# Attention and channel mix on one core: the second chunk in whole float32, and new due dates for the first four chunks

## The chip, the core and the metric

The kernel runs on one core of a Trainium2 chip. The core has a matrix engine (TensorE, "PE" in the profile, with its weight loads "PEld" shown apart), VectorE (DVE), ScalarE (ACT), GpSimd (POOL), and SyncE (SP), which here issues all loads and stores. The engines run side by side, each through its own queue in order, and wait for one another by semaphores. The metric is the device time of one execution in microseconds, lower is better. A difference of about 0.5% is what a measurement of this kernel can tell.

## The reference

Inputs q, k, v are 8 batches by 8 heads by 576 tokens by 64, in float32. Keys and values are averaged over groups of 8 tokens, so each head has 72 keys. Then comes a channel mix with weights w_k (512 x 1024), w_v (1024 x 512) and w_r (512 x 512):

```python
k_p = k.reshape(B, H, Sp, pool, D).mean(axis=3)
v_p = v.reshape(B, H, Sp, pool, D).mean(axis=3)
scores = scale * np.matmul(q, k_p.transpose(0, 1, 3, 2))
attn = softmax(scores)                     # written out in the reference
x = np.matmul(attn, v_p)                   # to [B, S, 512]
x_prev = np.concatenate([np.zeros((B, 1, D)), x[:, :-1, :]], axis=1)
xk = mu_k * x + (1.0 - mu_k) * x_prev
xr = mu_r * x + (1.0 - mu_r) * x_prev
k = np.maximum(xk @ w_k, 0.0)
v = k * k @ w_v
r = 1.0 / (1.0 + np.exp(-(xr @ w_r)))
out = (r * v).astype(np.float32)
```

## The kernel before

**Tiles and chunks.** The 4608 tokens are 36 tiles of 128 for attention and 13 chunks for the channel mix: chunk 0 has 128 tokens (tile 0), chunk 1 has 256 (tiles 1 and 2), the other eleven 384 (three tiles each).

**Stages of one chunk.** Scores and softmax per tile (`softmax`, `part`; `BY_HEAD` names the parts whose exponentials are taken head by head on ACT with the row sum beside it, in place of a subtraction and a row sum on DVE); `transposed` and `transposed_rest` turn the weights of a tile over; `attended` (L937) multiplies by the values for each of 4 groups of 128 channels; `shifted` (L950) and `joined` (L990) blend each token with the one before; `x_parts` (L1006, L1008) splits the result; `hidden` (L1034) multiplies by w_k in 8 blocks and squares the ReLU (L1043, L1050, then split at L1056 and L1058); `gate` (L1082) multiplies by w_r; `mixed` (L1115) multiplies by w_v; L1125 multiplies the two and L1129 stores.

**Two kinds of product.** A split product writes each operand as a high and a low part in float32r and runs three matmuls (high x high, low x high, high x low). A whole product is one matmul on plain float32, shown as two records. Chunk 0 is whole throughout (`WHOLE`), chunk 1 in the attention alone (`WHOLE_ATT`), everything else is split. In chunk 0, `joined` and `hidden` write their results straight into the operand, so there is nothing to split.

**Weights.** The 20 blocks of w_k, w_r and w_v arrive as pairs of words. `convert` rebuilds the float32 block in place (one ACT instruction, L528, two DVE instructions, L530 and L533). `split` then makes the high part on ACT (L555) and the low part on DVE or POOL (L558, by `LOW_BY`). There are 21 buffers for blocks; each split takes a new one and leaves the rebuilt block's to the next, so the splits run one after another in the order of the loads. A split waits for chunk 0's last use of the rebuilt block.

**Loads.** SP issues in the order of `LOADS`: k and v halves of a batch (two each), r (the remaining values), q (a tile's queries), c (constants), and the weight blocks. k, v and the second r need a buffer of the kind "stage". At first there are stage[0] and three early ones, lent by the split operands of later use (two in `sl`, one in `xrl`, the list `EARLY`). The early ones serve once; stage[0] returns as soon as its sums are done. A load without a buffer holds up everything behind it on SP. `SUM_BY` says who sums a half over its groups of 8: "t" PE by matmuls with the identity (L576), "v" DVE (L565, L607), "g" POOL.

**Order.** Every step is a small generator added with a due date. `Order.run` keeps a clock of its own with an estimated length for each instruction, and at each turn issues, on the engine that is free first, the ready step with the earliest due date. Due dates come from a formula plus the entry of `EARLIER` for the step's name. The estimates set only the order of the instructions, which is then fixed on each engine. `filling` gives 40 matmuls with no use, of late due date, for PE to run while nothing else is ready.

**Dependencies around the change.** `hidden` of chunk 2 starts after the last mix matmul of chunk 1, `gate` after all of its chunk's hidden, `mixed` after all of its chunk's gate. `attended` of chunk 2 needs chunk 1's gate to be done, since the operand buffer is the same. The operands of chunk 1 in `sl` and `xrl` wait for the early loads that lie in those buffers.

Of the kernel before, what the change touches and what calls it, by code (L numbers as in the profile page):

```python
# [34 lines left out]
WHOLE = (0,)  # L35
WHOLE_ATT = (0, 1)
# [9 lines left out]
    "k0 k1 k2 q0 r0 q1 c0 wk0 v0 k3 q2 wk1 wk2 wk3 wk4 v1 wk5 r1 q4 wk6 wk7 q3 v3 wr0 wr1 wr2 wr3 "  # L46
    "wv0 wv1 wv2 q5 wv3 wv4 wv5 wv6 wv7 v2 "
)

SUM_BY = {"k0": "t", "k1": "v", "v0": "t", "v1": "t", "r0": "t", "k2": "v", "k3": "v", "v2": "g", "v3": "v", "r1": "g"}  # L50
# [6 lines left out]
BY_HEAD = ((0, 1), (2, 0))  # L57
# [6 lines left out]
    "warm": 192.0, "constants": 417.1, "complements": 5357.6, "loads": 265.4, "keys 0 0": 155.5,  # L64
# [191 lines left out]
def attention_then_channel_mix(  # L256
# [55 lines left out]
    def operand(kind, c):  # L312
        if c in WHOLE:
            return whole_operands[kind]
        if (kind, c) not in operands:
            dtype = F32 if kind == "pth" and c in WHOLE_ATT else F32R
            operands[kind, c] = sb.tile(shapes[kind], dtype, name=f"{kind}_{c}", tag=kind)
        return operands[kind, c]
# [10 lines left out]
    def free_of_early(c, tag):  # L329
        return [("early", t, i) for t, n in EARLY for i in range(n) if t == tag and c not in WHOLE]  # L330

# [90 lines left out]
    def warm():  # L422

        zeros = yield take("tmp")
        yield "dve", 0.5, False
        nc.vector.memset(zeros, 0.0)
        bank = yield take("bank")
        for _ in range(WARMING):
            yield "pe", 0.86, False
            nc.tensor.matmul(out=bank[:, :256], lhsT=zeros[:, :P], rhs=zeros[:, :256], start=True, stop=True)  # L430
        order.give("bank", bank)
        order.give("tmp", zeros)
# [546 lines left out]
    def joined(c, g, m):  # L979
# [3 lines left out]
        if whole:  # L983
            xm = operand(f"x{'kr'[m]}h", c)[:, g]
            ts = xm[:, :n]
        else:
            xm = yield take("xm")
            ts = t[:, m, :n]
# [8 lines left out]
        if whole:  # L997
# [14 lines left out]
    def hidden(c, jt):  # L1012
        n = CHUNKS[c]
        whole = c in WHOLE
# [26 lines left out]
        rk = sh if whole else (yield take("rk"))  # L1041
# [12 lines left out]
        if not whole:  # L1054
# [9 lines left out]
    def gate(c, tt):  # L1064
        whole = c in WHOLE
# [21 lines left out]
        if last and whole:  # L1087
# [7 lines left out]
    def mixed(c, tt):  # L1095
        whole = c in WHOLE
# [6 lines left out]
        for jt in range(NJT):  # L1103
            yield need(("s", c, jt), ("full" if whole else "parts", "v", jt))
            yield pe(DM, whole, 1 if whole else 3)
            if jt == 0 and whole or jt == NJT - 1:
# [13 lines left out]
        if last and whole:  # L1120
# [26 lines left out]
    for kind, n in (("k", NJT), ("r", NCT), ("v", NJT)):  # L1147
        for i in range(n):
            at = {"k": FIRST + 2.6 * i - 4, "r": FIRST + 20 + 2 * i - 3, "v": FIRST + 28 + 2.5 * i}[kind]
            order.add(at, convert(kind, i))  # L1150
            used = [("hid", c, i) for c in WHOLE] if kind == "k" else [
# [75 lines left out]
```

## Time and profile before

| what | value |
|---|---|
| median of three timed executions | 641.62 us (641.49 to 643.84) |
| the profiled execution, whole | 642.56 us |
| its span, first to last instruction | 640.8 us |
| mean granted clock of TensorE | 1.000 |
| busy PE / PE weight loads | 622.0 / 552.0 us |
| busy DVE / ACT / POOL | 410.1 / 358.6 / 216.7 us |
| read from memory / written | 40.43 / 9.44 MB |

A group row of the profile reads: line, engine, operation, output <- inputs, partitions x elements and type, xcount | busy time in us, mean ns of one, then the idle time of the engine before them and what ended it. A timeline row reads: start, length, engine, line, operation, output <- inputs, count. Ends of matmuls are modelled, so a matmul's length includes the draining of the array; the pace of a row of matmuls is read from their starts. A DMA-issuing row of SP shows when the issue began, not the transfer.

### The profile page before, as it was taken

What the parts mean: (1) busy time and instruction counts of PE and PEld (TensorE: products, weight loads), DVE (VectorE), ACT (ScalarE), POOL (GpSimd) and SP (SyncE); (2) the same over time, 40 slices, a digit from 0 to 9 for tenths busy, and PEclk for the clock granted to TensorE, in tenths of its full rate; (3) what the DMA queues carried; (4) which work ended last, traced back from release to release, by engine and by line L of the source; (5) the groups of instructions that cost most, each with busy time, mean ns of one, the idle gap of its engine ahead of it and who ended that gap; (6) DMA issues with size and microseconds to landing.
All of it is one profiled execution on the core that took longest, in us unless ns stands there. A gap on an engine that the chain in (4) does not pass through costs nothing.

```text
span 640.8 us, 9433 instructions
## 1 busy us (share of the span) xinstructions
PE 622.0 (97%) x3411; PEld 552.0 (86%) x3411; DVE 410.1 (64%) x803; ACT 358.6 (56%) x788; POOL 216.7 (34%) x342
## 2 busy tenths in 40 slices
PE   9978899999999999999999999999999999999997
PEld 8866578888987987988988988988988988998986
DVE  5999998956946628925748735738965555553421
ACT  3888676666555557344665555554565456455320
POOL 1163338317416009204605106506605105203100
PEclk9999999999999999999999999999999999999999
DMA  9793341341321100530004100104111100000001
GB/s 338 257 389 121 92 143 46 97 136 64 109 74 50 50 1 18 173 90 34 18 27 163 58 16 34 34 25 166 58 21 38 42 17 18 34 0 17 34 1 50
DMA packets 19007, 50.48 MB, mean 79 GB/s; under 512 B 2256, under 2 KB 2512, under 8 KB 18960
## 3 DMA queue, kind: packets, MB, share of 16 engines
q1 hardware_dynamic: 18960, 49.87, 22.7%
q8 instruction: 27, 0.44, 0.3%
q14 instruction: 20, 0.16, 0.1%
HBM read 40.43 MB, written 9.44 MB: 78 GB/s over the span
## 4 chain that ended last, share of the span: by engine, by line
PE 78%; DVE 12%; ACT 4%; POOL 3%; DMA 2%; issue 1%; SPq 0%; DVEq 0%; POOLq 0%; ACTq 0%
PE mm L1034 27%; PE mm L1115 25%; PE mm L1082 15%; PE bank L937 4%; PE sc L735 4%; DVE xm L990 2%; PE bank L839 2%; POOL xkl L1008 1%; DVE sl L1058 1%; DMA got_wk<-in_w_k 1%; POOL xrl L1008 1%; PE bank L440 1%; ACT t L950 1%; DVE pr L876 1%; DVE stage L565 1%
## 5 line engine op out<-in xcount | busy, mean ns | idle before, releaser
L1034 PE MATMUL mm<-xkh,w_k 128*128 128x384 f32 (+1 forms) x768 | 194.3, 335 | 1.1 <-DVE rk L1050 1.1
L1115 PE MATMUL mm<-w_v,sh 128*128 128x512 f32 x560 | 186.7, 396 | 0.7 <-DVE w_v L558 0.7
L1034 PEld LDWEIGHTS mm<-xkh,w_k 128*128 128x128 f32 x768 | 136.2, 188 | 3.9 <-DVE rk L1050 2.2
L1034 PE MATMUL mm<-xkl,w_k 128*128 128x384 f32 (+1 forms) x384 | 126.9, 330 | 0.0
L1115 PEld LDWEIGHTS mm<-w_v,sh 128*128 128x128 f32 x560 | 105.4, 188 | 21.6 <-DVE w_v L558 1.2
L1115 PE MATMUL mm<-w_v,sl 128*128 128x512 f32 x280 | 109.3, 390 | 0.0
L1082 PE MATMUL mm<-w_r,xrh 128*128 128x512 f32 x280 | 90.8, 396 | 1.5 <-DVE rk L1050 1.5
L990 DVE SCALAR_TENSOR_TENSOR xm<-bank,given,t 128x384 f32<-128x384 f32 (+1 forms) x96 | 54.5, 601 | 44.9 <-POOL t L965 27.2
L1056 ACT CAST sh<-rk 128x384 fp32r<-128x384 f32 (+1 forms) x96 | 48.3, 505 | 57.9 <-DVE rk L1050 57.5
L1058 DVE TENSOR_TENSOR sl<-rk,sh 128x384 fp32r<-128x384 f32 (+1 forms) x96 | 57.1, 597 | 28.0 <-ACT sh L1056 27.4
L1008 POOL TENSOR_TENSOR xkl<-xm,xkh 128x384 fp32r<-128x384 f32 (+1 forms) x48 | 48.2, 1003 | 78.2 <-ACT xkh L1006 78.0
L1034 PEld LDWEIGHTS mm<-xkl,w_k 128*128 128x128 f32 x384 | 72.2, 188 | 0.1
L950 ACT ACTIVATE t<-bank,om_sb 128x384 f32<-128x384 f32 (+1 forms) x96 | 48.0, 570 | 39.2 <-PE bank L937 39.2
L797 POOL TENSOR_TENSOR px<-e,sm 128x64 f32<-128x64 f32 (+1 forms) x33 | 10.4, 314 | 160.3 <-DVE sm L791 150.5
L1043 ACT ACTIVATE rk<-mm 128x384 f32<-128x384 f32 (+1 forms) x96 | 46.0, 480 | 33.1 <-PE mm L1034 25.9
L1082 PEld LDWEIGHTS mm<-w_r,xrh 128*128 128x128 f32 x280 | 52.6, 188 | 12.7 <-DVE rk L1050 1.9
L1125 DVE TENSOR_TENSOR rs<-mm,rs 128x512 f32<-128x512 f32 x36 | 24.6, 684 | 60.3 <-PE mm L1115 60.1
L1050 DVE SCALAR_TENSOR_TENSOR rk<-mm,rk 128x384 f32<-128x384 f32 (+1 forms) x96 | 51.6, 540 | 17.9 <-ACT rk L1043 17.7
L1115 PEld LDWEIGHTS mm<-w_v,sl 128*128 128x128 f32 x280 | 52.8, 188 | 8.9
L1082 PE MATMUL mm<-w_r,xrl 128*128 128x512 f32 x140 | 54.6, 390 | 0.0
L565 POOL TENSOR_TENSOR stage<-stage 128x512 f32<-128x512 f32 (+5 forms) x57 | 48.6, 861 | 2.0
L1008 POOL TENSOR_TENSOR xrl<-xm,xrh 128x384 fp32r<-128x384 f32 (+1 forms) x48 | 48.1, 1002 | 2.5 <-ACT xrh L1006 2.4
(133 smaller groups left out, 926.3 us busy)
## 6 DMA issues: line engine op xcount, KB each, us to landing
qs<-in_qT SPq DMA_DIRECT2D x36, 256.0 KB, 3.4
out<-rs SPq DMA_DIRECT2D x36, 256.0 KB, 2.0
stage<-in_kT SPq DMA_DIRECT2D x14, 576.0 KB, 3.7
stage<-in_vm SPq DMA_DIRECT2D x15, 512.0 KB, 4.3
got_wk<-in_w_k SPq DMA_DIRECT2D x8, 512.0 KB, 6.9
got_wv<-in_w_v SPq DMA_DIRECT2D x8, 512.0 KB, 9.6
stage<-in_vr SPq DMA_DIRECT2D x6, 384.0 KB, 3.6
got_wr<-in_w_r SPq DMA_DIRECT2D x4, 512.0 KB, 8.9
```

Source lines behind the costliest of these rows:

```text
L565: nc_eng.tensor_tensor(out=st[:, :, :w], in0=st[:, :, :w], in1=st[:, :, w:2 * w], op=ALU.add)
L735: nc.tensor.matmul(out=halves[g // 2][o:o + n, 0, k:k + 2 * KEYS], lhsT=qs[:, g, o:o + n], rhs=kbd[b % 2][:, g, :], start=True, stop=True,)
L950: nc.scalar.activation(out=ts[m][:, 1:n + 1], in_=xp, func=AF.Copy, scale=om_sb[:, m, g:g + 1])
L990: nc.vector.scalar_tensor_tensor(out=xm[:, :n], in0=bank[:, :n], scalar=mu_sb[:, m, g:g + 1], in1=ts, op0=ALU.mult, op1=ALU.add,)
L1008: nc.gpsimd.tensor_tensor(out=lo, in0=xm[:, :n], in1=hi, op=ALU.subtract)
L1034: nc.tensor.matmul(out=hp, lhsT=w[:, o], rhs=x[:, ct, :n], start=(ct == 0 and k == 0), stop=(ct == NCT - 1 and k == len(terms) - 1),)
L1043: nc.scalar.activation(out=rk[:, :n], in_=hp, func=AF.Relu)
L1050: nc.vector.scalar_tensor_tensor(out=rk[:, :n], in0=hp, scalar=0.0, in1=rk[:, :n], op0=ALU.max, op1=ALU.mult)
L1056: nc.scalar.copy(out=sh[:, :n], in_=rk[:, :n])
L1058: nc.vector.tensor_tensor(out=operand("sl", c)[:, jt, :n], in0=rk[:, :n], in1=sh[:, :n], op=ALU.subtract)
L1082: nc.tensor.matmul(out=bank, lhsT=x[:, ct, o], rhs=w, start=(ct == 0 and k == 0), stop=(ct == NCT - 1 and k == len(terms) - 1),)
L1115: nc.tensor.matmul(out=bank, lhsT=s[:, o], rhs=w, start=(jt == 0 and k == 0), stop=(jt == NJT - 1 and k == len(terms) - 1),)
```

## The change

Chunk 1 (256 tokens) is computed in whole products in hidden, gate and mix as well, as chunk 0 is. Its blended inputs and its squares go straight into the operand buffers. The splits of the weights wait for chunk 1's use of the rebuilt blocks too. The early buffers are no longer waited for in chunk 1, which has no low parts. The order of loads is new; k2 is summed on POOL and not on DVE; tile 2's exponentials are no longer taken by head; the warm-up matmuls are estimated at half the length; all entries of `EARLIER` are new and cover chunks 0 to 3 and tiles 0 to 8 only, where before they covered chunk 4 and tiles 9 to 11 as well.

```diff
 WHOLE = (0,)
+WHOLE_HID = (0, 1)
+WHOLE_GATE = (0, 1)
+WHOLE_MIX = (0, 1)
 WHOLE_ATT = (0, 1)
...
 LOADS = (
-    "k0 k1 k2 q0 r0 q1 c0 wk0 v0 k3 q2 wk1 wk2 wk3 wk4 v1 wk5 r1 q4 wk6 wk7 q3 v3 wr0 wr1 wr2 wr3 "
-    "wv0 wv1 wv2 q5 wv3 wv4 wv5 wv6 wv7 v2 "
+    "k0 c0 r1 k1 r0 q0 wk0 q1 q2 v0 wk1 v1 wk2 q4 wk3 k2 wk4 q3 wk5 wk6 k3 wk7 wr0 wr1 wr2 wr3 v3 "
+    "wv2 wv0 wv1 wv3 q5 wv4 wv5 wv6 v2 wv7 "
 )
-SUM_BY = {"k0": "t", "k1": "v", "v0": "t", "v1": "t", "r0": "t", "k2": "v", "k3": "v", "v2": "g", "v3": "v", "r1": "g"}
+SUM_BY = {"k0": "t", "k1": "v", "v0": "t", "v1": "t", "r0": "t", "k2": "g", "k3": "v", "v2": "g", "v3": "v", "r1": "g"}
...
-BY_HEAD = ((0, 1), (2, 0))
+BY_HEAD = ((0, 1),)
...
 EARLIER = {
-    "warm": 192.0, "constants": 417.1, "complements": 5357.6, "loads": 265.4, "keys 0 0": 155.5,
...
+    "filling": 216.2, "last_values 1": 228.8, "convert k 0": 201.7, "split k 0": 26.7, "convert k 1": 32.6,
...
 }
...
     def operand(kind, c):
...
-            dtype = F32 if kind == "pth" and c in WHOLE_ATT else F32R
+            whole = {"pth": WHOLE_ATT, "xkh": WHOLE_HID, "xrh": WHOLE_GATE, "sh": WHOLE_MIX}.get(kind, ())
+            dtype = F32 if c in whole else F32R
...
     def free_of_early(c, tag):
-        return [("early", t, i) for t, n in EARLY for i in range(n) if t == tag and c not in WHOLE]
+        kept = c in {"sl": WHOLE_MIX, "xrl": WHOLE_GATE}[tag]
+        return [("early", t, i) for t, n in EARLY for i in range(n) if t == tag and not kept]
...
         for _ in range(WARMING):
-            yield "pe", 0.86, False
+            yield "pe", 0.43, False
...
     def joined(c, g, m):
...
-        if whole:
+        direct = c in (WHOLE_GATE if m else WHOLE_HID)
+        if direct:
             xm = operand(f"x{'kr'[m]}h", c)[:, g]
-            ts = xm[:, :n]
+            ts = xm[:, :n] if whole else t[:, m, :n]
...
-        if whole:
+        if direct:
             order.make(("x", c, g, m))
         else:
             order.add(att_due[c] + g, x_parts(c, g, m, xm))
...
     def hidden(c, jt):
-        whole = c in WHOLE
+        whole = c in WHOLE_HID
...
-        rk = sh if whole else (yield take("rk"))
+        kept = c in WHOLE_MIX
+        rk = sh if kept else (yield take("rk"))
...
     def gate(c, tt):
-        whole = c in WHOLE
+        whole = c in WHOLE_GATE
...
     def mixed(c, tt):
-        whole = c in WHOLE
+        whole = c in WHOLE_MIX
...
-            used = [("hid", c, i) for c in WHOLE] if kind == "k" else [
-                k for c in WHOLE for k in every({"r": "gated", "v": "mixed"}[kind], c)
+            used = [("hid", c, i) for c in WHOLE_HID] if kind == "k" else [
+                k for c in {"r": WHOLE_GATE, "v": WHOLE_MIX}[kind]
+                for k in every({"r": "gated", "v": "mixed"}[kind], c)
             ]
```

More of the change, by code (lines that the diff above doesn't have):

```diff
@@ L63 @@
 EARLIER = {
-    "warm": 192.0, "constants": 417.1, "complements": 5357.6, "loads": 265.4, "keys 0 0": 155.5,
[51 rows of a table removed]
[14 rows of a table added]
+    "warm": 295.8, "constants": 172.6, "complements": 249.6, "loads": 162.3, "keys 0 0": 279.4,
[26 rows of a table added]
 }
@@ L1053, in hidden @@
             order.give("mm", bank)
-        if not whole:
+        if not kept:
             yield act(n)
@@ L1086, in gate @@
         order.make(("gated", c, tt))
-        if last and whole:
+        if last and c in WHOLE:
             order.give("stage", stage[1])
@@ L1105, in mixed @@
             yield pe(DM, whole, 1 if whole else 3)
-            if jt == 0 and whole or jt == NJT - 1:
+            if jt == 0 and c in WHOLE or jt == NJT - 1:
                 order.make(("mixing", c, tt))
@@ L1119, in mixed @@
         order.make(("mixed", c, tt))
-        if last and whole:
+        if last and c in WHOLE:
             order.give("stage", stage[2])
```

90 rows, old and new, of the table EARLIER are left out of this document.

## The prediction, made before the changed kernel was seen

> **What bounds the kernel now.** I read the windows of the whole span first, then the chain of waits at its end, then what TensorE (PE) waited for in the early part, then the queue of loads (SP) and the single instructions behind it.
>
> ```profile
> span 640.8 us, 9433 instructions
> 0.00:30.00 30.00, 27.78 (x203) 26.16 (x204) 23.22 (x70) 18.05 (x61) 6.14 (x23) 1.00 0.84 301
> 30.00:60.00 30.00, 25.49 (x171) 20.48 (x171) 28.92 (x57) 26.04 (x64) 15.43 (x20) 1.00 0.73 267
> 60.00:90.00 30.00, 25.59 (x135) 18.86 (x133) 29.43 (x62) 19.35 (x44) 9.85 (x10) 1.00 0.37 119
> 90.00:120.00 30.00, 27.68 (x162) 24.51 (x161) 26.21 (x43) 20.73 (x46) 22.03 (x36) 1.00 0.23 73
> 120.00:200.00 80.00, 79.35 (x429) 70.38 (x428) 54.15 (x115) 48.59 (x99) 28.05 (x41) 1.00 0.30 95
> 200.00:600.00 400.00, 399.23 (x2145) 359.30 (x2144) 238.16 (x444) 217.11 (x462) 135.19 (x214) 1.00 0.14 48
> 600.00:641.00 41.00, 36.91 (x180) 32.31 (x178) 9.97 (x18) 8.77 (x17) 0.00 (x0) 1.00 0.05 20
> ```
>
> The columns after the length are busy PE, PE weight loads, VectorE (DVE), ScalarE (ACT), GpSimd (POOL), then the granted clock, the DMA share and GB/s. From 120 us on PE is busy for all but 1.4 of 480 us: there the time is the matmuls themselves, and nothing but fewer matmuls shortens it. Before 120 us DVE is the fullest engine (28.9 and 29.4 of 30 us in the second and third windows), and PE pauses for 4.5, 4.4 and 2.3 us. The clock is 1.00 throughout. So the change can gain only in the first 120 us, and what it adds to PE counts in full unless it fills a pause.
>
> ```profile
> 595.73 16.66 PE mm L1034 x96
> 612.39 8.20 PE mm L1082 x36
> PE mm L1034 <- ACT stage L1043: 2.7, 2, 1.4
> PE bank L894 <- DVE pr L876: 1.6, 3, 1.1
> PE mm L1082 <- DVE rk L1050: 1.5, 1, 1.5
> PE mm L1115 <- DVE got_wv L533: 1.2, 1, 1.2
> PE mm L1034 <- DVE rk L1050: 1.1, 2, 0.8
> PE mm L1115 <- DVE w_v L558: 0.7, 1, 0.7
> PE mm L1115 <- DVE rk L1050: 0.4, 1, 0.4
> ```
>
> The first two rows are the end of the chain: a split chunk of 384 tokens costs 16.66 us of hidden matmuls and 36 gate matmuls 8.20 us, 0.228 each. The others are PE's waits between 28.9 and 120 us (total us, times, longest). The view's eleven rows add up to 11.1 us; these seven are 9.2 of it. Chunk 1's squares (rk, 3.0 us in three rows), chunk 0's ReLU behind a crowded ACT (2.7), the rebuilt and split w_v (1.9) and the softmax leftovers (1.6) are the pauses.
>
> **The change, part by part.**
>
> *Dearer matmuls in chunk 1.* It has 32 hidden products (8 blocks by 4) on 256 columns and 24 gate and mix products (2 by 4, 2 by 8) on 512. Each was three split matmuls and becomes one whole product, which the profile shows as two records.
>
> ```profile
> 50.56 0.40 PE L1034 MATMUL mm<-xkh,w_k 128*128 128x256 f32 x2
> 50.80 0.28 PE L1034 MATMUL mm<-xkl,w_k 128*128 128x256 f32 x1
> 50.92 0.40 PE L1034 MATMUL mm<-xkh,w_k 128*128 128x256 f32 x2
> 57.03 0.80 PE L1034 MATMUL mm<-xkh,w_k 128*128 128x256 f32 x2
> 52.39 3.70 PE L1082 MATMUL mm<-got_wr,stage 128*128 128x512 f32 x8
> L1082 PE MATMUL mm<-got_wr,stage 128*128 128x512 f32 x8 | 3.7, 605 | 0.1
> 35.82 2.01 PE L1034 MATMUL mm<-stage,got_wk 128*128 128x128 f32 x16
> ```
>
> A split trio of 256 columns takes 50.92 - 50.56 = 0.36 us. Eight whole records of 512 columns take 3.70 us with the last one's 0.605 us of draining, so (3.70 - 0.605) / 7 = 0.442 each, 0.884 a product, against 3 x 0.228 = 0.683 split. Whole records of 256 columns on weights are not shown; half of 0.442 is 0.221, and twice the 128-column pace (2.01 / 16 = 0.126) is 0.25. I take 0.225, nearer the first because the second still holds a drain: 0.45 a product. Added: 32 x 0.09 + 24 x 0.201 = 2.9 + 4.8 = **+7.7 us** of PE (bounds 7.4 to 9.3).
> The Trainium skill, "FP8 and Floating Point Precision", section "TensorE Precision Notes", has true float32 as four passes through the array. By passes alone a whole product would cost 4/3 of a trio, an estimate of 32 x 0.12 + 24 x 0.228 = 9.3 us; the rows of chunk 0 give 0.884 against 0.683, a ratio of 1.29, so the measured pace is taken.
>
> *An earlier start.* The order of loads moves v1, the second half of the first batch's values, ahead of four w_k blocks and k3.
>
> ```profile
> 8.28 0.33 SPq L511 DMA_DIRECT2D stage<-in_kT  x1
> 18.28 0.33 SPq L511 DMA_DIRECT2D stage<-in_vm  x1
> 19.02 0.37 ACT L891 CAST whole_ptr<-bank 96x256 fp32r<-96x256 f32 x1
> 23.05 1.95 PE L576 MATMUL mm<-stage,ident 128*128 128x128 f32 x16
> 26.00 0.39 PE L937 MATMUL bank<-whole_pth,vbd_w 128*128 128x128 f32 x2
> 28.91 0.39 PE L1034 MATMUL mm<-stage,got_wk 128*128 128x128 f32 x2
> L440 PE MATMUL bank<-ident 128*128 128x128 f32 x80 | 10.3, 276 | 0.0
> ```
>
> Only stage[0] is used again in this phase. It goes to k3 at 8.28, and v1, next in line for it, cannot be issued before 18.28; its sums run at 23.05, attention of chunk 0 at 26.00, hidden at 28.91. Tile 0's softmax was ready at 19.02 + 0.37 = 19.4. In the new order r1, k1 and v0 take the three early buffers and v1 takes stage[0] straight after k0, at about 8.3. Attention can then begin at about 19.6, up to 6.4 us sooner. What hides it: PE has nothing else there but 10.3 us of filler matmuls. Next late are the w_k blocks that v1 displaced and k2, k3, which now wait for stage[0] in the same SP queue, with w_k4 and w_k7 and all of w_r and w_v queued behind them. So not all arrives: I take **-5.5 us** (bounds 0 and -6.4).
> k2's sum moves from DVE, where it ran in a slack stretch, to POOL: its 1.9 us on DVE were free, and on POOL it may cost something.
>
> ```profile
> 7.97 1.25 DVE L565 TENSOR_TENSOR early_sl<-early_sl 128x576 f32<-128x576 f32 x2
> 41.48 2.90 DVE L533 SCALAR_TENSOR_TENSOR got_wr<-got_wr,tmp 128x512 int32<-128x512 int32 x2
> 42.11 1.72 POOL L558 TENSOR_TENSOR w_k<-got_wk,w_k 128x512 fp32r<-128x512 f32 x1
> ```
>
> Two DVE instructions took 2.90 us while POOL subtracted for 1.72. Three such halvings on POOL (576, 288 and 2 x 144 columns, 3.9 us at that pace) can hold up DVE by 0 to 3.9 us; 1 taken inside the sums below.
> The Trainium skill, "SBUF — State Buffer", section "SBUF: two separate sides", calls the port pair that VectorE and GpSimd share an exclusive lock held for a whole instruction. The two rows agree; by the rule the sum of k2 would cost up to its full 3.9 us, and the eight x_parts subtractions that vanish from POOL would give more than that back.
>
> *DVE, ACT and POOL relieved.* For chunk 1 the eight casts and eight POOL subtractions of x_parts vanish, and with them eight casts (L1056) and eight DVE subtractions (L1058) of the squares. The split of the 20 weight blocks is no longer needed before chunk 2.
>
> ```profile
> L1058 DVE TENSOR_TENSOR sl<-rk,sh 128x256 fp32r<-128x256 f32 x8 | 4.4, 551 | 0.0
> L555 ACT CAST w_v<-got_wv x8: 602/616/629, 75.4 to 93.9; 128x512 fp32r<-128x512 f32 x8
> L558 POOL TENSOR_TENSOR w_v<-got_wv,w_v x4: 1287/1316/1501, 76.1 to 92.1; 128x512 fp32r<-128x512 f32 x4
> L558 DVE TENSOR_TENSOR w_v<-got_wv,w_v x4: 680/687/1566, 79.7 to 94.7; 128x512 fp32r<-128x512 f32 x4
> L776 DVE TENSOR_TENSOR e<-sc,mx 128x576 f32<-128x576 f32 x33 | 24.9, 753 | 1.3
> L784 DVE TENSOR_REDUCE sm<-e 128x8 f32<-128x576 f32 x34 | 25.3, 745 | 16.5 <-ACT e L782 16.4
> ```
>
> DVE loses 4.4 us (L1058), and four w_v subtractions of 0.69 or more, 2.8 to 3.6, slide behind chunk 1. It gains tile 2's subtraction and row sum, 0.75 + 0.75, since tile 2's exponentials are no longer taken by head on ACT. Net about -6 us of DVE before chunk 2. Which pauses go: I drop those of chunk 0's ReLU (2.7), the squares (3.0), w_v (1.9), together **-7.6 us**, and keep the other 3.5. The squares' DVE step itself stays, so 3.0 is the least sure; if DVE still lags, it returns (bounds -4 and -11.1). Changes between whole and split matmuls also cost: the pair at 57.03 takes 0.80 where the same pair takes 0.40, and such pairs stand at each hand-over of chunks 0 and 1. With both whole, **-1.5 us** (bounds 0 and -3).
>
> *A new wait.* A split of block i now needs chunk 1's use of it as well; the splits go one after another, since each needs the buffer that the one before released. The eight of w_v start only after chunk 1's last mix product. Queued behind is mix of chunk 2, and behind that hidden of chunk 3. It is due after hidden and gate of chunk 2, 16.66 + 8.20 = 24.9 us later. The chain's own length is 8 x 0.62 + 4 x 1.32 + 4 x 0.69 = 13 us, 15 with hand-overs; in the profile it took 75.4 to about 95.4, 20 us. It fits, but it loads DVE, ACT and POOL while chunk 3's softmax is due: **+1.5 us** (bounds 0 and 8).
>
> The estimates of time in the scheduling code (0.43 for 0.86 in the warm-up) change only order. Chunk 4's dates falling back to the formula costs nothing: later chunks already run by it in the full window of 200 to 600.
>
> *Sum:* 640.8 + 7.7 - 5.5 - 7.6 - 1.5 + 1.5 = 635.4 us of span. The profiled execution took 642.56, 1.76 more than its span, and lies 0.94 above the median of 641.62. With 1.76 - 0.94 = 0.8 added, the time comparable to the median is **636.2 us**.
>
> **The rivals.**
> *PE nearly full (chance 0.17).* If hidden of chunk 1 fills every gap, all 11.1 us of pauses go and the start gives 6.4: 640.8 + 7.7 - 6.4 - 11.1 - 1.5 + 0.8 = 630.3. For it: chunk 1 then needs nothing but rebuilt weights, and has some 35 us of ready PE work. Against it: DVE was 97% full there and still has to rebuild 20 blocks.
> *DVE goes on setting the pace (0.22).* Then only what DVE no longer does counts, 6 us, the early start runs into the same queue, and the dearer matmuls eat it: 640.8 + 7.7 - 6 - 1.5 + 0.8 = 641.8, no change that can be told. For it: DVE's two full windows. Against it: in 90 to 120 DVE had 3.8 us idle, and softmax work for later tiles was already being done ahead.
> *The w_v splits come late (0.14).* If each of the eight links waits about 2 us in the queues of DVE and ACT, the chain takes 15 + 16 = 31 us, 6 over the 25 it has, and PE stands before chunk 2's mix with nothing else ready; the crowding also keeps 3 us of the pauses: 636.2 + 6 + 3 = 645.2, slower. It decides from a chain of 25 us on. For it: one of the four DVE links above took 1.57. Against it: these splits' due dates lie earlier than chunk 2's.
>
> **How the numbers follow.** Forecast 636.2 (chance 0.47); rivals 630.3 (0.17), 641.8 (0.22), 645.2 (0.14). The range 629.5 to 643 takes in the first three and leaves out the slow rival's upper part and little below. A measurement of this kernel tells about 0.5%, 3.2 us, from no change: faster is below 638.4, slower above 644.8. The forecast's case with its spread lies nearly all below 638.4, with the fast rival 0.63; the same 0.24; slower 0.13.
>
> **What would show it.** Right: attention of chunk 0 (L937) near 20 us and its hidden near 22 to 23; chunk 1's hidden as 64 records of about 0.22; PE idle between 30 and 120 of some 5 us; the eight w_v splits after chunk 1's mix and done within 25 us. Wrong at the start: v1 still issued after 15 us. Wrong in the pauses: PE still waiting for rk or got_wv by more than 4 us. Wrong in the chain: PE waiting for w_v before chunk 2's mix. Wrong in all: a pace of whole matmuls other than 0.44 for 512 columns, or a granted clock below 1.00.

## The result, and the profile after

The changed kernel takes 631.53 us (median of four executions, 631.29 to 632.17), the kernel before in the same job 641.64. The ratio is 0.9836, 95% interval 0.9814 to 0.9858: 10.1 us faster. The forecast was 636.2, with a range of 629.5 to 643. The profiled execution of the changed kernel took 631.48 us, close to the median, and its span is 11.1 us shorter than that of before; one of these 11.1 us is that the profiled execution of before lay 0.94 above its own median.

First the page of the changed kernel and its windows over the whole span, in the columns of the prediction's first fence (busy PE, weight loads, DVE, ACT, POOL, granted clock, DMA share, GB/s).

```profile
span 629.7 us, 9238 instructions
PE 622.3 (99%) x3355; PEld 548.0 (87%) x3355; DVE 394.2 (63%) x792; ACT 350.9 (56%) x755; POOL 215.3 (34%) x338
...
L1111 PE MATMUL mm<-w_v,sh 128*128 128x512 f32 x528 | 173.3, 394 | 0.0
```

```profile
0.00:30.00 30.00, 27.97 (x211) 26.71 (x212) 21.91 (x63) 16.09 (x47) 9.53 (x27) 1.00 0.74 272
30.00:60.00 30.00, 29.01 (x177) 24.71 (x177) 28.29 (x66) 21.88 (x55) 5.64 (x11) 1.00 0.78 282
60.00:90.00 30.00, 29.74 (x113) 16.40 (x112) 24.61 (x54) 23.68 (x44) 15.40 (x20) 1.00 0.45 160
90.00:120.00 30.00, 29.80 (x165) 25.94 (x164) 26.80 (x53) 21.20 (x49) 20.40 (x27) 1.00 0.13 47
120.00:200.00 80.00, 80.00 (x419) 70.65 (x418) 50.73 (x105) 42.03 (x88) 29.55 (x44) 1.00 0.30 102
200.00:600.00 400.00, 400.00 (x2165) 362.34 (x2165) 237.76 (x450) 222.66 (x470) 134.75 (x211) 1.00 0.14 47
```

PE's busy total hardly moved (622.0 to 622.3): dearer matmuls came in, slow restarts went out. What went is idle time. In the three windows from 30 to 120 PE stood still for 4.51, 4.41 and 2.32 us before and for 0.99, 0.26 and 0.20 now; from 120 to 600 for 1.42 and now for nothing. DVE still fills 28.29 of 30 us in the second window, and PE stands still there for only 0.99.

PE's waits in the changed kernel between 20 and 125 us (total us, times, longest) are these four and no more, 1.5 us against 11.1 before:

```profile
PE mm L1029 <- DVE sh L1046: 0.5, 1, 0.5
PE mm L1029 <- DVE xkh L985: 0.5, 1, 0.5
PE mm L1111 <- ACT rs L1086: 0.3, 1, 0.3
PE bank L888 <- DVE pr L870: 0.2, 1, 0.2
```

From the timeline of the changed kernel (start, length, engine, line, operation): the loads of v1 and k2, the last copy of v1's sums, the last cast of tile 0's softmax, the first attention and hidden product of chunk 0, chunk 1's hidden and gate, the first hidden product of chunk 2. Line numbers have shifted: L1029, L1078, L1111 and L931 were L1034, L1082, L1115 and L937.

```profile
9.68 0.33 SPq L505 DMA_DIRECT2D stage<-in_vm  x1
...
19.87 0.33 SPq L505 DMA_DIRECT2D stage<-in_kT  x1
...
20.62 0.53 ACT L627 COPY vbd_w<-mm 64x128 f32<-64x128 f32 x2
...
21.18 0.37 ACT L885 CAST whole_ptr<-bank 96x256 fp32r<-96x256 f32 x1
...
21.24 0.39 PE L931 MATMUL bank<-whole_pth,vbd_w 128*128 128x128 f32 x2
...
23.95 0.49 PE L1029 MATMUL mm<-stage,got_wk 128*128 128x128 f32 x2
...
40.54 7.17 PE L1029 MATMUL mm<-xkh,got_wk 128*128 128x256 f32 x32 [0.47 <-DVE xkh L985]
...
59.85 5.31 PE L1078 MATMUL mm<-got_wr,xrh 128*128 128x512 f32 x12
...
96.79 0.60 PE L1029 MATMUL mm<-xkh,w_k 128*128 128x384 f32 x2
```

The chain of w_v splits, from the tile view of w_v in the changed kernel (count: shortest, median, longest ns, first to last start):

```profile
L549 ACT CAST w_v<-got_wv x8: 602/622/627, 100.3 to 123.5; 128x512 fp32r<-128x512 f32 x8
L552 DVE TENSOR_TENSOR w_v<-got_wv,w_v x4: 641/683/694, 104.5 to 124.6; 128x512 fp32r<-128x512 f32 x4
L552 POOL TENSOR_TENSOR w_v<-got_wv,w_v x4: 1277/1290/1759, 106.0 to 121.2; 128x512 fp32r<-128x512 f32 x4
```

It now runs from 100.3 to 125.3, after chunk 1's mix as predicted, and the mix of chunk 2, which uses these blocks, starts at 126.8.

**A balance of PE's time.** Idle time undercounts what PE loses, since a restart after a pause also lengthens a matmul (in before, 0.50 us for the gate product at 78.03, after 1.46 us of waiting, and 0.39 for its like a little later). So I gave every matmul of the traces the pace that its kind keeps in an undisturbed row (split: 0.227 us for 512 columns, 0.174 for 384; whole: 0.431 for 512, 0.217 for 256; fillers nothing) and called the rest of the span lost. The rows above give the two whole paces within 1%: (7.17 - 0.38) / 31 = 0.219 and (5.31 - 0.6) / 11 = 0.428.

| us | before | after | e2 | e10 | e11 | e12 | e1 | e8 |
|---|---|---|---|---|---|---|---|---|
| matmuls at their own pace | 600.5 | 607.2 | 607.2 | 607.2 | 607.2 | 607.2 | 600.5 | 604.3 |
| lost, 0 to 30 | 16.7 | 14.9 | 16.5 | 16.7 | 12.6 | 13.7 | 15.3 | 15.3 |
| lost, 30 to 120 | 16.1 | 2.5 | 7.7 | 7.0 | 9.7 | 7.5 | 37.7 | 32.1 |
| lost, 120 to 600 | 3.3 | 0.9 | 6.3 | 0.9 | 3.1 | 1.6 | 10.1 | 5.0 |
| lost, from 600 on | 4.2 | 4.2 | 4.1 | 4.6 | 4.2 | 4.2 | 4.3 | 4.2 |

Before to after: +6.7 of matmuls, -1.8, -13.6, -2.5 and 0, together -11.1 (-11.2 with the rounding of the rows). The other columns belong to the runs below.

### The profile page after: what moved, and what is told of

Its sections match the earlier page's. It is cut to its first block, busy times and chain, and to the rows that moved or that the text cites. A ratio compares the mean times of both kernels' runs of the same rounds, so it can differ in the third digit from the quotient of the medians.

```text
span 629.7 us, 9238 instructions
## 1 busy us (share of the span) xinstructions
PE 622.3 (99%) x3355; PEld 548.0 (87%) x3355; DVE 394.2 (63%) x792; ACT 350.9 (56%) x755; POOL 215.3 (34%) x338
## 4 chain that ended last, share of the span: by engine, by line
PE 88%; ACT 3%; DVE 3%; POOL 3%; DMA 2%; issue 1%; SPq 0%; POOLq 0%; ACTq 0%; DVEq 0%
PE mm L1029 30%; PE mm L1111 29%; PE mm L1078 16%; PE bank L931 5%; PE sc L729 4%; PE bank L833 2%; DMA got_wr<-in_w_r 1%; DMA stage<-in_kT 1%; PE bank L424 1%; PE bank L434 1%; PE bank L888 1%; POOL stage L559 1%; ACT e L776 0%; ACT tmp L522 0%; DVE got_wk L527 0%
## 5 line engine op out<-in xcount | busy, mean ns | idle before, releaser
L1029 PE MATMUL mm<-xkh,w_k 128*128 128x384 f32 x704 | 180.9, 337 | 0.0
L1111 PE MATMUL mm<-w_v,sh 128*128 128x512 f32 x528 | 173.3, 394 | 0.0
L1029 PEld LDWEIGHTS mm<-xkh,w_k 128*128 128x128 f32 x704 | 126.0, 188 | 1.0 <-issue 0.6
L1029 PE MATMUL mm<-xkl,w_k 128*128 128x384 f32 x352 | 117.7, 335 | 0.0
L1111 PEld LDWEIGHTS mm<-w_v,sh 128*128 128x128 f32 x528 | 99.3, 188 | 19.4
L1111 PE MATMUL mm<-w_v,sl 128*128 128x512 f32 x264 | 103.0, 390 | 0.0
L1078 PE MATMUL mm<-w_r,xrh 128*128 128x512 f32 x264 | 86.0, 397 | 0.0
L985 DVE SCALAR_TENSOR_TENSOR xm<-bank,given,t 128x384 f32<-128x384 f32 x88 | 50.6, 612 | 40.2 <-POOL t L959 23.0
L1052 ACT CAST sh<-rk 128x384 fp32r<-128x384 f32 x88 | 45.0, 513 | 50.2 <-DVE rk L1046 50.0
L1054 DVE TENSOR_TENSOR sl<-rk,sh 128x384 fp32r<-128x384 f32 x88 | 51.9, 592 | 24.8 <-ACT sh L1052 24.4
L1029 PEld LDWEIGHTS mm<-xkl,w_k 128*128 128x128 f32 x352 | 66.1, 188 | 0.0
L1046 DVE SCALAR_TENSOR_TENSOR rk<-mm,rk 128x384 f32<-128x384 f32 x88 | 48.6, 553 | 17.4 <-ACT rk L1039 17.0
L1078 PEld LDWEIGHTS mm<-w_r,xrh 128*128 128x128 f32 x264 | 49.6, 188 | 10.2
L1003 POOL TENSOR_TENSOR xkl<-xm,xkh 128x384 fp32r<-128x384 f32 x44 | 44.7, 1017 | 37.2 <-ACT xkh L1001 37.1
L1111 PEld LDWEIGHTS mm<-w_v,sl 128*128 128x128 f32 x264 | 49.7, 188 | 8.7
L559 POOL TENSOR_TENSOR stage<-stage 128x512 f32<-128x512 f32 (+7 forms) x59 | 51.3, 878 | 13.7 <-DVE w_k L552 11.4
L1039 ACT ACTIVATE rk<-mm 128x384 f32<-128x384 f32 x88 | 43.0, 489 | 20.9 <-PE mm L1029 19.9
L1078 PE MATMUL mm<-w_r,xrl 128*128 128x512 f32 x132 | 51.4, 389 | 0.0
L1003 POOL TENSOR_TENSOR xrl<-xm,xrh 128x384 fp32r<-128x384 f32 x44 | 44.8, 1019 | 1.3 <-ACT xrh L1001 1.2
```

The source lines that it names most:

```text
L559: nc_eng.tensor_tensor(out=st[:, :, :w], in0=st[:, :, :w], in1=st[:, :, w:2 * w], op=ALU.add)
L985: nc.vector.scalar_tensor_tensor(out=xm[:, :n], in0=bank[:, :n], scalar=mu_sb[:, m, g:g + 1], in1=ts, op0=ALU.mult, op1=ALU.add,)
L1003: nc.gpsimd.tensor_tensor(out=lo, in0=xm[:, :n], in1=hi, op=ALU.subtract)
L1029: nc.tensor.matmul(out=hp, lhsT=w[:, o], rhs=x[:, ct, :n], start=(ct == 0 and k == 0), stop=(ct == NCT - 1 and k == len(terms) - 1),)
L1039: nc.scalar.activation(out=rk[:, :n], in_=hp, func=AF.Relu)
L1046: nc.vector.scalar_tensor_tensor(out=rk[:, :n], in0=hp, scalar=0.0, in1=rk[:, :n], op0=ALU.max, op1=ALU.mult)
```

## The experiments

Two theories at first. A: whole products take conversions, subtractions and the early need for split weights off DVE, ACT and POOL, and so PE stops pausing. B: the gain comes from the new order of loads and the new due dates, and whole products only cost. A third, L, came with the first results: what matters within the order is which loads SP issues first. Unless said otherwise an edit is made in the changed kernel.

### e1: new loads and dates, chunk 1 split

```diff
-WHOLE_HID = (0, 1)
-WHOLE_GATE = (0, 1)
-WHOLE_MIX = (0, 1)
+WHOLE_HID = (0,)
+WHOLE_GATE = (0,)
+WHOLE_MIX = (0,)
```

> Changed kernel with chunk 1 split again in hidden, gate and mix; the new loads, sums and due dates stay (x_parts of chunk 1 have no date of their own and fall back to the formula). Theory A, the whole products free chunk 1 of the weight splits and this is the gain: TensorE gets 6.7 us less work but its pauses before 120 us come back (8 to 11 us in place of 1.5), span 632 to 640. Theory B, the gain is the new order of loads and the new dates alone: the pauses stay away and the span falls by the 6.7 us of dearer matmuls, to about 623.

669.89 us, ratio 1.0432 (1.0394 to 1.047). Two windows and two of PE's waits of e1:

```profile
60.00:90.00 30.00, 19.03 (x73) 12.36 (x73) 27.91 (x57) 18.46 (x38) 6.75 (x7) 0.83 0.44 160
90.00:120.00 30.00, 19.05 (x119) 16.40 (x117) 20.63 (x38) 20.10 (x40) 20.52 (x33) 0.87 0.25 80
```

```profile
PE sc L729 <- DVE e L770: 7.5, 4, 2.2
PE bank L888 <- DVE pr L870: 6.8, 1, 6.8
```

PE is idle for 11 of 30 us in both windows, 13.0 of the 22 us behind DVE's softmax steps. The new loads and dates with chunk 1 split are 28 us worse than before, so theory B falls; theory A had the sign but allowed a span of only 632 to 640. That the dates fit a DVE that has no chunk 1 to split is the likely reason, but e1 doesn't show it apart.

### e2: whole products in the kernel before, nothing else

Loads, sums, by-head parts, dates and the warm-up's estimate stay as before; against the kernel before:

```diff
 WHOLE = (0,)
+WHOLE_HID = (0, 1)
+WHOLE_GATE = (0, 1)
+WHOLE_MIX = (0, 1)
```

> Kernel before with chunk 1 in whole products alone; old loads, sums, heads and due dates. Theory A: most pauses between 30 and 120 us go although the dates are the old ones, hidden of chunk 0 starts at about 29 us as before, span 632 to 637. Theory B: pauses as before (11 us) and 6.7 us more matmuls, span about 647.

644.18 us, ratio 1.0036 (1.0021 to 1.0051): no gain either, and a span of 641.8 about midway between the two theories. Windows of e2:

```profile
30.00:60.00 30.00, 25.65 (x156) 21.01 (x155) 29.02 (x64) 22.16 (x54) 11.17 (x14) 1.00 0.76 288
60.00:90.00 30.00, 30.00 (x110) 17.50 (x108) 18.46 (x45) 18.83 (x40) 6.48 (x10) 1.00 0.34 106
90.00:120.00 30.00, 28.20 (x151) 23.54 (x150) 22.12 (x37) 19.41 (x42) 20.07 (x28) 1.00 0.15 52
120.00:200.00 80.00, 77.17 (x412) 66.86 (x411) 57.81 (x120) 49.95 (x101) 32.35 (x47) 1.00 0.31 100
```

The mechanism of theory A is there: from 60 to 90 DVE falls from 29.43 to 18.46 and PE never stops. But chunk 0 starts as late as before, so 30 to 60 keeps its 4.35 us of idle PE while DVE stays full, and 2.83 turn up between 120 and 200, where PE waits above all for POOL's low parts of a chunk's inputs (1.0) and for DVE's softmax (0.9). By the balance e2 loses 34.6 us in all where before loses 40.3: 5.7 won, and the matmuls are 6.7 dearer.

### e3, e4, e5 and e9: loads and products without any due-date corrections

With `EARLIER` empty all due dates come from the formula, so that loads and products can be compared without a table that was fitted to one of them. The sums, the by-head part and the warm-up's estimate are those of the changed kernel in all four.

```diff
-EARLIER = {
...
-}
+EARLIER = {}
```

> Changed kernel with all entries of EARLIER taken out: order by the formula alone. Theory A: the whole products give slack, so that the untuned order costs little, span 633 to 640, and below the next kernel's by at least 4 us. Theory B: the dates are the gain, span 641 or more, and no better than the next kernel's.

> As the kernel without dates, but with chunk 1 split in hidden, gate and mix: both differ in the whole products alone. Theory A: the split chunk stalls for its weight splits, span 640 to 650, at least 4 us above the whole one. Theory B: 6.7 us below the whole one.

> Changed kernel without the entries of EARLIER and with the old order of loads; against the kernel without dates (633.5 us) it differs in LOADS alone. Theory L, the order of loads is a part of the gain of its own: v1 is issued at about 18 again, hidden of chunk 0 starts near 29, 638 us or more. Theory W, with whole products the order of loads matters little: within 2 us of 633.5.

> Chunk 1 split, old order of loads, no entries of EARLIER: the fourth corner beside 633.5 (whole, new loads), 646.2 (whole, old loads) and 660.2 (split, new loads). If whole products and the loads each act on their own (the loads 12.7 us, the products 26.7 us, in different stretches of time), about 673. If they shorten the same waits, less than that, 655 to 666.

| median us, no corrections | old loads | new loads | loads give |
|---|---|---|---|
| chunk 1 split | 664.39 (e9) | 660.18 (e4) | -4.2 |
| chunk 1 whole | 646.20 (e5) | 633.52 (e3) | -12.7 |
| whole gives | -18.2 | -26.7 | |

Each part helps, and together they help by 8.5 us more than the sum of the two alone. Part of every difference in the table is TensorE's clock and not waiting: the mean granted clock was 0.97 in e9, 0.98 in e4, 0.99 in e5 and 1.00 in e3, and how much that makes was not worked out. Of the expectations, e4's missed: its span of 658.8 lies 9 us above the range. e3's of 631.7 lies 1 us below, and in e5 v1 went out at 30 us and not at 18.

With both parts and no table at all, e3 is 8.1 us faster than the kernel before (641.59 in the same job). The corrections then give the changed kernel only 2.0 us more (633.52 to 631.53); with split products the difference between e9 and the kernel before is 22.8 us, which I put down mostly to its table (the by-head part, k2's sum and the warm-up's estimate differ as well, and were not tried apart). My reading of why e2 shows no gain while e9 to e5 shows 18 is that the table of before had already repaired by hand most of what whole products would repair; no run shows that by itself.

What the old order costs in e5 is shown by its queue of loads and by one wait of PE:

```profile
30.09 0.33 SPq L463 DMA_DIRECT2D stage<-in_vm  x1
```

```profile
PE mm L528 <- DMA stage<-in_vm: 7.2, 1, 7.2
```

v1 goes out at 30.09, as it waits for stage[0] behind k3 (16.4 us of that for k3's sums on DVE), and PE waits 7.2 us for it.

### e10: v1 alone moved up

In e5, v1 is put right behind v0 and nothing else is changed.

```diff
-"... wk0 v0 k3 q2 wk1 wk2 wk3 wk4 v1 wk5 ..."
+"... wk0 v0 v1 k3 q2 wk1 wk2 wk3 wk4 wk5 ..."
```

> Changed kernel without the entries of EARLIER, old order of loads with one move: v1 directly behind v0, ahead of k3. If v1's place is what the new order brings at the start, as the forecast held, most of the 12.7 us between 646.2 and 633.5 is won: 633 to 637, attention of chunk 0 at 20 to 22. If it is the place of k2, r1 or the weights, 641 or more.

638.13 us, ratio 0.9942 (0.9918 to 0.9965), 8.1 less than e5. The two loads in its queue:

```profile
9.89 0.33 SPq L463 DMA_DIRECT2D stage<-in_vm  x1
...
19.91 0.33 SPq L463 DMA_DIRECT2D stage<-in_kT  x1
```

v1 leaves at 9.89, k3 waits for stage[0] until 19.91 in its stead, and that costs less. One load's place makes 8.1 of the 12.7 us of the whole order: theory L holds for this load. The clock has a share in this too (0.86 from 30 to 60 us in e5, 0.94 in e10).

### e6: all w_v low parts on POOL; e7: k2 summed on DVE

In both, the order of all instructions is held to that of the changed kernel, so that only the engine changes.

```diff
-LOW_BY = {"k": "gvgvvvgv", "r": "gvgv", "v": "gvvggvgv"}
+LOW_BY = {"k": "gvgvvvgv", "r": "gvgv", "v": "gggggggg"}
```

> Changed kernel with all eight low parts of w_v on GpSimd, every engine's steps held in the changed kernel's order. The chain of w_v splits grows by 4 x 0.6 = 2.4 us. In the changed kernel it ends at 125.3 and mix of chunk 2 starts at 126.8 with block 2 first needed and block 7 last. If the chain has slack, as the forecast held, TensorE does not wait and the time stays within 1 us of 631.5; if it is at its edge (the slow rival), TensorE waits before or in chunk 2's mix and the time grows by 2 to 4 us.

```diff
-SUM_BY = {... "k2": "g", ...}
+SUM_BY = {... "k2": "v", ...}
```

> Changed kernel with k2 summed on VectorE again, every engine's steps held in the changed kernel's order. If the sum on GpSimd is what holds stage[0], k3, w_k7 and w_r behind it in the SP queue are issued about 2 us sooner (k3 at 27 in place of 29.1) and the time falls by up to 1 us; if VectorE is the tighter resource there, the 1.9 us on it cost 0 to 2 us.

e6: 632.80 us, ratio 0.9843 (0.9782 to 0.9904). e7: 632.06, ratio 0.9832 (0.9771 to 0.9892). Neither can be told from 631.53; e6 lies between the two cases that its expectation named. The chain in e6, from its tile view:

```profile
L549 ACT CAST w_v<-got_wv x8: 602/620/626, 99.8 to 125.8; 128x512 fp32r<-128x512 f32 x8
L552 POOL TENSOR_TENSOR w_v<-got_wv,w_v x8: 1282/1426/1664, 103.6 to 126.5; 128x512 fp32r<-128x512 f32 x8
```

Its last low part begins at 126.5 and takes over 1.28, so the chain lasts about 28 us in place of 25, and PE has no wait for w_v even so. In e7 k3 is issued at 29.47 against 29.06, so it was not POOL's sum of k2 that held stage[0] up. The prediction allowed 0 to 3.9 us for k2's sum on POOL; moving it back to DVE changes nothing that these runs can tell. By the lock on the shared port in the Trainium skill ("SBUF — State Buffer", "SBUF: two separate sides") it could have been the upper end; if the lock held anything up here, these runs don't show it in the time.

### e8: only the mix of chunk 1 split

```diff
-WHOLE_MIX = (0, 1)
+WHOLE_MIX = (0,)
```

> Changed kernel with chunk 1's mix split again (hidden and gate stay whole; x_parts vanish still, squares are split again). If the w_v splits ahead of chunk 1's mix are the main stall that the change removes, more than half of the 38 us between the split and the whole kernel with the new dates come back: 650 or more. If the stalls lie at hidden and gate, 631 to 640.

663.37 us, ratio 1.0319 (1.025 to 1.0388). Tile view of w_v, a wait of PE, and windows of 4 us of e8:

```profile
L549 ACT CAST w_v<-got_wv x8: 617/618/620, 112.7 to 125.6; 128x512 fp32r<-128x512 f32 x8
```

```profile
PE mm L1111 <- ACT w_v L549: 5.5, 1, 5.5
```

```profile
98.00:102.00 4.00, 1.20 (x3) 0.72 (x4) 3.42 (x10) 2.06 (x8) 3.39 (x6) 0.50 0.50 147
...
110.00:114.00 4.00, 0.00 (x0) 0.00 (x0) 3.91 (x8) 1.77 (x5) 1.77 (x3) 0.84 0.50 155
...
118.00:122.00 4.00, 4.00 (x11) 2.93 (x9) 2.58 (x6) 1.24 (x2) 2.47 (x2) 0.50 0.44 137
...
126.00:130.00 4.00, 4.00 (x24) 3.19 (x21) 1.39 (x2) 0.22 (x1) 0.00 (x0) 1.00 0.31 108
```

Chunk 1's mix now needs the split w_v, which stand in the serial chain behind the splits of w_k and w_r. Chunk 1's gate was done at 71.7, but the first split of w_r began at 92.3, and its low part ran on POOL only at 105.5. The time falls in the case "650 or more", yet the run doesn't price the mix alone; it shows what the chain costs once PE has little else to do: 32.1 us lost between 30 and 120. Part whole is worse here than all whole, and (by before's 641.6) worse than all split with a table of its own.

### e11 and e12: two more orders of loads with tables of their own

Is there time left in the first 30 us? Both change `LOADS` and `EARLIER` only. Cut to the first loads:

```diff
-"k0 c0 r1 k1 r0 q0 wk0 q1 q2 v0 wk1 v1 wk2 q4 wk3 k2 wk4 q3 wk5 wk6 k3 wk7 ..."
+"k0 r1 c0 k1 r0 q0 wk0 q1 v0 wk1 v1 wk2 wk3 q4 q2 k2 wk4 q3 wr1 wk5 wk7 wk6 ..."   (e11)
+"k0 c0 r1 k1 r0 q0 wk0 v0 q1 wk1 v1 q4 q2 wk2 k2 wk3 wk4 q3 wk6 wk5 q5 k3 ..."     (e12)
```

> The changed kernel with another order of loads and another table of due dates: the blocks of w_k 2 and 3 and the first values go ahead of the queries 4 and 2 and of the keys 2, part of w_r and w_v ahead of the keys 3 and values 3. Nothing that is computed changes. In the changed kernel TensorE had lost 22.5 us to anything but matmuls, 14.9 of them in the first 30 us and 4.1 at the end, 3.5 between. If the first 30 us can still be shortened by an earlier start of the attention and of the hidden products (21.24 and 23.95 us): 628 to 630.5 us. If the start is set by the softmax's chain and the rest is matmuls: within 1.5 us of 631.5, and new due dates have nothing left to win.

> A second such order and table: the values 0 go ahead of the queries 1, the queries 2 come behind the values 1 and the queries 4, and the keys 3 ahead of all of w_r. Same two expectations: 628 to 630.5 us if the first 30 us still hold time that an order can win, within 1.5 us of 631.5 if not.

e11: 639.40 us, ratio 0.9961 (0.9946 to 0.9976). e12: 634.47, ratio 0.9879 (0.9863 to 0.9896). Neither expectation came true: both are slower than the changed kernel. Timeline of e11 (first attention of chunk 0, first hidden product, a gate product with the idle time before it):

```profile
19.83 0.39 PE L1047 MATMUL bank<-whole_pth,vbd_w 128*128 128x128 f32 x2
...
22.21 0.71 PE L1145 MATMUL mm<-stage,got_wk 128*128 128x128 f32 x4
...
51.97 1.13 PE L1194 MATMUL mm<-got_wr,stage 128*128 128x512 f32 x2 [1.52 <-DVE got_wr L643]
```

The start did come earlier, 19.83 and 22.21 for 21.24 and 23.95, and 2.3 us less was lost by 30 us. Between 30 and 120 it lost 9.7 for 2.5, with no single large wait: rebuilt w_r blocks (1.5), softmax leftovers, rebuilt w_v. An early start gains nothing on balance if the blocks and softmaxes behind it come later.

## Why the prediction was right, and where its sizes were wrong

The sign, the range and the place of the gain (before 120 us) were right, and the likeliest case was 4.7 us too slow. What came true is nearest to the first rival, PE nearly full, at 630.3. That the sum came within 4.7 us is in part luck, since the start brought 3.7 us less than forecast and the other three steps together 9.5 us more (a net 5.8 of span, of which 0.94 is only that the profiled execution of before lay above its median). By its own steps, in us:

| step | forecast | measured |
|---|---|---|
| dearer matmuls | +7.7 (7.4 to 9.3) | +6.7 |
| earlier start | -5.5 (0 to -6.4) | -1.8 by 30 us |
| pauses and restarts, 30 to 120 | -7.6 - 1.5 | -13.6 |
| new wait for w_v, and beyond 120 | +1.5 (0 to 8) | -2.5 |

**Dearer matmuls.** Right in kind, 1 us too high and below the lower bound. The paces are 0.428 for 0.442 and 0.219 for 0.225; the row of before that the prediction used starts slowly, with 0.53 us from its first record to its second (52.39 to 52.93) and 0.429 for each of the rest, and the mean of the seven hid that. The ratio to three split matmuls is 2 x 0.428 / 0.683 = 1.25, where the prediction's estimate by the four passes of the Trainium skill ("FP8 and Floating Point Precision", "TensorE Precision Notes") gave 4/3.

**Earlier start.** v1 went out at 9.68, 8.6 us sooner (the forecast had it at about 8.3). Attention moved from 26.00 to 21.24 and not to 19.6: v1's sums were copied by 21.15, and the softmax of tile 0 ended later, its last cast at 21.18 where it was 19.02. The first product doesn't read that cast; the next one waited 0.16 us for it. Hidden moved from 28.91 to 23.95, by 5.0. That is near the 5.5, but PE had done only 1.8 us more of matmuls by 30 us; the rest shows as pauses that are gone after 30. The step that failed is to price this edit by the start alone and to add it to the others. The 8.1 us of e5 to e10 can't be set against the bound of 6.4, since v1 moved by 20.2 us there (30.09 to 9.89) and by 8.6 here; what v1's place alone is worth in the changed kernel was not run.

**Pauses.** The three named ones went (ReLU of chunk 0, w_v, and the squares but for 0.5 us), and so did most of the 3.5 us that the prediction kept for the softmax and the rest: 1.5 of 11.1 are left in all. It kept them because DVE looked full. DVE has 79.7 us of work from 30 to 120 (28.29 + 24.61 + 26.80) for 84.6 before, and the forecast relief of 6 us compares with 4.9 here and 1.3 before 30 (k2's 1.9 among them). But with whole products PE holds a long stretch of work that needs only rebuilt weights (the row of 32 records at 40.54 runs through with no pause), so a late DVE hardly stops it; this is read from the rows and was not tested apart. Restarts weren't measured apart from the pauses.

**The new wait.** Order and length were right (25 us, after chunk 1's mix), the cost was not: no wait of PE for w_v, and from 120 to 600 less is lost than before. In the rival's condition, a chain of over 25 us, e6 had some 28 us and came out 1.3 above, with no wait for w_v: the threshold was set too low. Between the first hidden product of chunk 2 (96.79) and its mix (126.8) lie 30 us and not 24.9, since PE does other work in between.

**DVE sets the pace** (641.8): fell, by the four waits of PE above. **Whole products as the cause:** needed with the tables at hand, and not enough. e2 has them without the loads and gains nothing, e1 has the loads and table without them and loses 28 us; e3 has both without any table and gains 8.1 of the 10.1. What stays open is why the tables of e11 and e12 do worse, load by load, and whether a table made for whole products on the old loads, or for split products on the new ones, would gain: neither was run.

## What to carry to other kernels

A table of due dates is fitted to the work it orders, so a part of a change that is tried without a new table (e2), or a table without its part (e1), says little of either; compare both without the table first, as e3, e4, e5 and e9 do. When two edits remove the same kind of pause from the engine that bounds, don't add their gains: here they gave 8.5 us more together than apart, and the clock's share in that is open. In an in-order queue of loads, look for the load that waits for a buffer ahead of what the first compute needs: one such place was worth 8 us in a kernel without due-date corrections.

## What the runs showed of the hardware

Pauses of TensorE can be paid twice. In before and in the changed kernel the granted clock is 1.00 in every window up to 600 us. In the experiments that pause more it falls where PE pauses: 0.83 and 0.87 in e1's two windows above, and in e8's windows of 4 us it stands at 0.50 from 98 to 106 and again from 114 to 122, though PE is busy in all of the last four. There the matmuls take nearly twice their time: the last two rows below start 0.43 us apart, where such products keep 0.227 elsewhere, and the first is 0.79 us long against the mean of 394 ns that the page of the changed kernel gives for this group.

```profile
114.94 0.79 PE L1111 MATMUL mm<-w_v,sh 128*128 128x512 f32 x1 [5.48 <-ACT w_v L549]
...
119.27 0.63 PE L1111 MATMUL mm<-w_v,sl 128*128 128x512 f32 x1
119.70 0.63 PE L1111 MATMUL mm<-w_v,sh 128*128 128x512 f32 x1
```

So part of the 20 us and more by which e1 and e8 lie above before is clock and not waiting; how much was not worked out. Not every pause does this: e11 loses 9.7 us between 30 and 120 and keeps 1.00 in its windows there. The Trainium skill ("TensorE: Matmul & The Clock Gate", "Part 1: The HAM clock gate (the "warmup" mystery)") has the clock halve after an idle window of about 3.4 us and come back after a busy one of about that length; the row at 114.94, after 5.48 us of idling, agrees with the first half. The return agrees as far as windows of 4 us can tell: PE was busy throughout 118 to 122 at 0.50, and the window from 126 has 1.00.
